# Two sliding-window attention layers, twice: products, sums and places of VectorE and GpSimd assigned anew

## The chip, the cores and the metric

The kernel runs on one core of a Trainium2 chip. The metric is the device time of one execution in microseconds (us). Below, PE is TensorE (matrix products), ACT is ScalarE, DVE is VectorE, POOL is GpSimd, and SP issues the transfers.

## The reference

Four layers act on x of 2048 tokens by 512 features, in the order A, B, A, B, and each adds its result to x. Each starts with a layer norm and ends with a product with its wo. Both layer types have 32 heads of 16 features.

```python
def _A_ref(x, wqkv, wo):                 # W, dil = 8, 2
    idx = pos[:, None] - (jnp.arange(W) * dil)[None, :]
    logits = jnp.einsum("bhsd,bhswd->bhsw", q, kg) * scale
    logits = jnp.where(mask[None, None, :, :], logits, -1e9)
    attn = _softmax(logits, axis=-1)
    o = jnp.einsum("bhsw,bhswd->bhsd", attn, vg)
...
def _B_ref(x, wqkv, wo):                 # W = 256
    scores = jnp.einsum("bhqd,bhkd->bhqk", q, k) * (Dh ** -0.5)
    mask = (idx[:, None] - idx[None, :] >= 0) & (idx[:, None] - idx[None, :] < W)
    p = _softmax(jnp.where(mask[None, None], scores, -1e9), axis=-1)
    o = jnp.einsum("bhqk,bhkd->bhqd", p, v)
...
x = x + _A_ref(_layernorm(x, axis=-1), A_wqkv, A_wo)
x = x + _B_ref(_layernorm(x, axis=-1), B_wqkv, B_wo)
x = x + _A_ref(_layernorm(x, axis=-1), A_wqkv, A_wo)
x = x + _B_ref(_layernorm(x, axis=-1), B_wqkv, B_wo)
```

In a layer A each token attends to 8 tokens, 2 apart. In a layer B it attends to the last 256 tokens.

## The kernel before, in words

The tokens are cut into 8 chunks of 256. A chunk passes through an A layer and then through the next B layer. With two pairs of layers this makes 16 A parts, named A0 to A15, and 16 B parts, B0 to B15. Features lie on the 128 partitions, in four blocks m.

**An A part** (`layer_a`, L836). After the norm and the three projections (L766 to L768), the logits are made in 16 pieces. One `prod` (L893, instruction L895) multiplies q by 8 shifted views of k: 64 tokens by 8 offsets, 512 values on each partition, from SBUF and into SBUF (tile `pr`, four buffers). For each m, four of them feed `reduce_` on PE (L903), which sums over a head's features into the PSUM tile L. `top` (L926, L927) and `bottom` (L930 to L932) on DVE and two steps on ACT make the softmax; `erest` (L940) is the low half of its split into two float16 tiles. Then `spread` (L962) puts the weights on all feature rows in PSUM (tile `pb`), `weigh` (L975, always DVE, 1,024 values) multiplies them by the 8 views of v into tile `pw` (three buffers), and `total` (L977) sums the 8 offsets by three additions in place, L979, L980 and L981, of 512, 256 and 128 values. There are 8 pairs of `weigh` and `total` in an A part. `finish` (L796) splits the sum (L805 on ACT; L807, the low half `ol`), multiplies by wo (L785 to L787) and adds to x (L813).

**A B part** (`layer_b`, L988). Scores go twice through PE. The first time (L1067, L1070) they are there for the row maxima alone, which DVE takes (`top`: L1086 and L1088, or L1081 in a first chunk); `msplit` (L1097, L1098) cuts the maxima in two. The second time (L1140, L1142) they come out transposed, less the maxima, and go to the exponential on ACT (L1146), the mask on POOL (L1155) and the product with v on PE (L1172). Both kinds of scores share two PSUM buffers (`q_sc`). At the end a multiplication of 512 values (L1246) divides by the sums, and `finish` follows.

**The order** is written out in a table. Each step is a task of a `Plan` with an engine and a cost in us. `ORDER` (L40) gives, for each task of each part, its place in its engine's sequence. Four kinds of tasks (`prod`, `total`, `erest`, `ol`) and L1246 have an alternative engine: a negative entry in the table sends the task there. `Plan.order` (L431) runs the sequences against the costs and gives the order in which instructions are emitted, and with it the rotation of the tiles' buffers; each engine keeps the table's order. Tasks of neighbouring parts are mixed: while A4 makes its logits, PE also runs scores of B2 and B3. In the table, DVE has 160 `prod`, POOL 96; POOL has 97 `total`, DVE 31.

In this model of costs a task of mode "S" (a DVE or POOL task between SBUF tiles) is lengthened by 0.7 (DVE) or 0.35 (POOL) of the time that a task of that mode on the other engine lies beside it.

Of the kernel before, what the change touches and what calls it, by code (L numbers as in the profile page):

```python
# [11 lines left out]
F32 = mybir.dt.float32  # L12
# [6 lines left out]
P = 128  # L19
# [21 lines left out]
    "pA": [1, 0, 2, 1, 0, 1, 3, 3, 4, 9, 8, 7, 6, 4, 4, 3, 3, 6, 5, 7, 9, 10, 16, 14, 13, 13, 12, 8, 10, 5, 5, 10, 4,  # L41
        11, 14, 14, 18, 17, 17, 15, 6, 12, 9, 16, 23, 22, 23, 36, 27, 32, 26, 31, 25, 33],
    "pB": [10, 22, 12, 21, 33, 34, 28, 47, 35, 39, 74, 33, 39, 13, 30, 11, 29, 55, 49, 37, 59, 41, 66, 41, 67, 38, 65,
        17, 35, 14, 37, 64, 63, 44, 73, 50, 49, 73, 42, 72, 16, 32, 7, 15, 69, 75, 51, 81, 54, 71, 51, 88, 43, 56, 23,
        24, 44, 15, 20, 21, 19, 18],
    "W": [8, 43, 46, 50, 48, 52, 51, 57, 54, 60, 61, 53, 65, 67, 66, 68, 45, 74, 82, 71, 79, 77, 90, 76, 70, 80, 105,
        88, 96, 91, 83, 102, 104, 99, 97, 106, 101, 108, 84, 113, 98, 109, 112, 111, 100, 103, 166, 169, 181, 190,
        173, 187, 186, 198, 195, 189, 192, 196, 197, 202, 201, 203, 230, 209, 225, 221, 227, 236, 319, 322, 2496,
        2503, 2518, 2522, 2524, 2535, 2531, 2538, 2539, 2546, 2552, 2542, 2554, 2543, 2558, 2563, 2567, 2589, 2596,
        2610, 2609, 2615, 2618, 2632, 2623, 2625, 2622, 2621, 2635, 2628, 2629, 2627, 2624, 2626, 2631, 2634, 2630,  # L50
        2636, 2633, 2645],
    "A0": [0, 1, 0, 1, 2, 2, 2, 6, 5, 8, 7, 11, 9, 2, 0, 11, 12, 13, 19, 20, 21, 25, 27, 20, 23, 15, 16, 17, 18, 24,
        28, 29, 30, 19, 24, 32, 35, 44, 56, 38, 39, 40, 41, 36, 27, 7, 11, 18, -4, -5, 19, 26, 22, 20, -6, 21, 31, -7,
        24, 25, 26, 37, 30, -9, 29, -10, 42, 28, 10, 34, 31, 36, 34, 38, 58, 40, 12, 42, 13, 62, 43, 14, 45, -47, 72,
        48, -50, 47, 16, 78, 52, 18, 53, -56, 40, 17, 85, 86, 87, 89, 58, 44, -58, 92, 93, 94, 95, 61],
    "B0": [59, 62, 21, 64, 46, 110, 48, 69, 45, 107, 47, 68, 115, 117, 120, 122, 114, 116, 118, 119, 54, 77, 52, 75,
        22, 26, 29, 23, 27, 25, 30, 40, 42, 39, 126, 129, 130, 139, 123, 124, 125, 128, 60, 83, 57, 79, 31, 32, 34,
        33, 36, 35, 37, 38, 41, 43, 162, 163, 164, 167, 66, 176, 177, 179, 180, 68, 174, 107, 161, 99, 168, 101, 155,
        96, 153, 92, 170, 103, 159, 97, 175, 105, 108, 184, 114, 45, 212, 73, 204, 70, 35, 220, 206, 71, 217, 74, 36,
        224, 83, 200, 122, 210, 126, 194, 121, 188, 113, 191, 116, 208, 124, 183, 111, 182, 117, 127, 215, 129, 46,  # L60
        235, 80, 231, 78, 40, 252, 258, 88, 266, 91, 42, 289, 101, 234, 141, 241, 147, 216, 131, 228, 138, 226, 137,
        237, 143, 232, 139, 222, 136, 148, 251, 151, 51, 290, 98, 287, 97, 49, 332, 281, 94, 296, 99, 51, 334, 111,
        223, 134, 250, 154, 280, 164, 262, 157, 259, 156, 265, 160, 249, 153, 240, 144, 168, 294, 173, 64, 305, 102,
        302, 100, 52, 310, 311, 109, 318, 108, 54, 329, 110, 67, 66, 72, 73, 204, 74, 75, 212, -66, 122, -216, 363,
        364, 365, 366, 221, 78, 124, 66, 367, 370, 372, 373, 224, 77],
    "A1": [15, 63, 60, 22, 70, 50, 121, 53, 76, 55, 127, 56, 78, 20, 19, 131, 132, 134, 138, 140, 141, 143, 146, 59,
        61, 133, 135, 136, 137, 142, 145, 147, 148, 58, 62, 150, 151, 152, 157, 156, 158, 165, 171, 63, 67, 26, 38,
        82, 81, -25, 80, 144, 86, 87, 84, 85, 149, 90, -26, 89, 91, 154, -28, 93, 94, 95, 160, 98, 64, 100, 65, 102,
        172, 104, 28, 106, 29, 178, 110, 30, 109, -116, 185, 112, 31, 119, 34, 193, 118, 33, 120, -124, 69, 32, 199,
        205, 207, 211, 128, 72, -126, 213, 214, 218, 219, 132],  # L70
    "B1": [130, 133, 39, 135, 75, 229, 77, 140, 76, 233, 79, 142, 239, 243, 246, 247, 238, 242, 244, 245, 84, 152, 81,
        150, 47, 49, 53, 52, 50, 48, 54, 63, 69, 65, 254, 257, 263, 264, 248, 253, 256, 260, 90, 161, 89, 159, 57, 55,
        58, 56, 60, 59, 61, 62, 68, 70, 308, 309, 314, 315, 106, 320, 325, 326, 327, 112, 316, 185, 295, 174, 303,
        179, 291, 171, 286, 169, 306, 181, 312, 183, 321, 188, 189, 331, 193, 71, 347, 118, 337, 114, 61, 351, 340,
        116, 349, 120, 62, 360, 342, 117, 338, 115, 63, 377, 358, 123, 352, 121, 69, 378, 131, 335, 197, 348, 207,
        330, 198, 328, 195, 346, 205, 343, 203, 323, 191, 339, 201, 210, 359, 214, 76, 379, 132, 369, 126, 71, 394,
        374, 130, 385, 133, 72, 396, 416, 146, 392, 135, 74, 431, 393, 136, 406, 142, 75, 438, 153, 362, 218, 388,
        229, 384, 228, 381, 227, 361, 219, 353, 211, 368, 222, 375, 225, 230, 395, 235, 84, 424, 149, 412, 144, 78,
        446, 443, 155, 434, 152, 81, 459, 440, 154, 457, 158, 86, 463, 452, 157, 449, 156, 84, 467, 165, 407, 240,
        397, 237, 417, 245, 433, 254, 425, 248, 430, 249, 398, 238, 411, 243, 255, 445, 258, 99, 461, 161, 464, 162,  # L80
        88, 477, 468, 166, 472, 167, 89, 483, 478, 168, 481, 171, 92, 492, 484, 172, 480, 170, 93, 493, 173, 98, 97,
        106, 105, 288, 107, 108, 295, -104, 184, 105, 524, 525, 526, 527, 305, 110, 186, 107, 528, 532, 533, 534, 307,
        111],
    "A2": [28, 145, 146, 41, 149, 82, 255, 85, 155, 86, 261, 87, 158, 37, 48, 267, 268, 269, 274, 275, 276, 278, 279,
        93, 95, 270, 271, 272, 273, 277, 283, 284, 285, 92, 96, 292, 293, 298, 300, 299, 301, 307, 313, 105, 107, 50,
        64, 163, -45, -44, 162, 282, 166, 167, -46, 165, 288, -48, 172, -47, 170, 297, 178, 175, 177, 176, 304, 180,
        103, 182, 104, 184, 317, 186, 53, 187, 55, 324, 192, 56, 190, -195, 333, 196, 57, 199, 59, 336, 200, 60, 202,
        -207, 113, 58, 341, 344, 345, 350, 209, 119, -209, 354, 355, 356, 357, 216],
    "B2": [213, 217, 68, 220, 125, 371, 127, 223, 128, 376, 129, 226, 382, 386, 390, 391, 380, 383, 387, 389, 137,
        236, 134, 233, 80, 82, 85, 86, 83, 81, 87, 96, 103, 100, 401, 405, 409, 410, 399, 400, 402, 404, 145, 244,  # L90
        141, 242, 90, 88, 91, 89, 93, 92, 94, 95, 101, 102, 462, 470, 474, 475, 169, 482, 486, 489, 494, 175, 473,
        270, 453, 263, 458, 265, 448, 260, 444, 259, 465, 267, 469, 268, 476, 272, 273, 487, 277, 104, 506, 180, 496,
        176, 99, 511, 499, 177, 509, 182, 101, 519, 503, 179, 500, 178, 102, 521, 518, 185, 512, 183, 109, 538, 194,
        495, 282, 508, 291, 491, 281, 488, 279, 505, 289, 501, 287, 485, 276, 497, 284, 293, 520, 299, 109, 539, 193,
        530, 189, 110, 554, 535, 191, 544, 195, 111, 555, 578, 208, 548, 196, 113, 593, 553, 198, 566, 203, 114, 594,
        215, 523, 301, 549, 314, 543, 311, 540, 310, 522, 303, 513, 296, 529, 304, 536, 308, 315, 556, 318, 113, 584,
        211, 572, 206, 118, 606, 603, 217, 596, 212, 122, 618, 595, 216, 616, 221, 124, 626, 612, 219, 609, 218, 123,
        633, 230, 565, 323, 557, 319, 579, 328, 590, 333, 585, 329, 591, 332, 558, 321, 571, 325, 337, 605, 344, 132,
        620, 223, 625, 225, 125, 637, 628, 227, 631, 228, 126, 640, 634, 229, 642, 233, 129, 651, 644, 234, 639, 232,
        130, 654, 235, 131, 130, 137, 138, 371, 139, 141, -141, 378, 246, 143, 684, 685, 686, 687, 388, 143, 248,  # L100
        -385, 689, 692, 693, 694, 391, 144],
    "A3": [79, 232, 231, 73, 234, 138, 403, 139, 239, 140, 408, 143, 241, 67, 70, 413, 414, 419, 423, 422, 427, 428,
        436, 148, 150, 415, 418, 420, 421, 426, 429, 435, 437, 147, 151, 441, 442, 450, 454, 451, 455, 460, 466, 159,
        164, 85, 100, 247, -78, -77, 246, 432, 251, 253, 250, 252, 439, -81, 257, -80, 256, 447, -83, 262, 261, -84,
# [1216 lines left out]
```

## Time and profile before

| | |
|---|---|
| median of 3 runs | 1564.64 us (1563.51 to 1567.54) |
| the profiled execution | 1569.09 us |
| span from its first to its last instruction | 1567.3 us |
| mean granted clock of PE | 0.941 |
| instructions | 35,200 |
| ACT busy | 732.7 us |
| transfers | 96.34 MB, mean 61 GB/s |

The span is what the profile's views cover; the execution's own time is 1.8 us more, and 4.45 us over the median. "Busy" is the time in which an engine runs an instruction. The profile counts a PE instruction as busy over its modelled length, so at a lower granted clock the same work is more busy time.

### The profile page before, as it was taken

What the parts mean: (1) busy time and instruction counts of PE and PEld (TensorE: products, weight loads), DVE (VectorE), ACT (ScalarE), POOL (GpSimd) and SP (SyncE); (2) the same over time, 40 slices, a digit from 0 to 9 for tenths busy, and PEclk for the clock granted to TensorE, in tenths of its full rate; (3) what the DMA queues carried; (4) which work ended last, traced back from release to release, by engine and by line L of the source; (5) the groups of instructions that cost most, each with busy time, mean ns of one, the idle gap of its engine ahead of it and who ended that gap; (6) DMA issues with size and microseconds to landing.
All of it is one profiled execution on the core that took longest, in us unless ns stands there. A gap on an engine that the chain in (4) does not pass through costs nothing.

```text
span 1567.3 us, 35200 instructions
## 1 busy us (share of the span) xinstructions
PE 1419.5 (91%) x14186; PEld 804.5 (51%) x14186; DVE 1295.9 (83%) x2386; ACT 732.7 (47%) x1011; POOL 777.2 (50%) x806
## 2 busy tenths in 40 slices
PE   6899979989899998989899898989989899898988
PEld 4473636446373644636455463735536364463534
DVE  6868797987979798897987979797897979889774
ACT  6432434444445444444455343545444454454554
POOL 3414253654846275573636537363564636547233
PEclk9798999989999999989899898988999899998999
DMA  6130122112130311212122221202212221221211
GB/s 215 28 96 20 62 50 72 48 48 69 50 89 20 96 40 55 79 33 89 29 69 60 60 79 33 88 21 84 54 41 76 50 89 25 64 75 33 82 44 42
DMA packets 73091, 96.34 MB, mean 61 GB/s; under 512 B 17120, under 2 KB 44256, under 8 KB 72928
## 3 DMA queue, kind: packets, MB, share of 16 engines
q1 hardware_dynamic: 72672, 93.83, 21.1%
q8 instruction: 111, 1.82, 0.5%
q14 instruction: 52, 0.43, 0.1%
q10 hardware_dynamic: 256, 0.26, 0.1%
HBM read 49.81 MB, written 34.05 MB: 54 GB/s over the span
## 4 chain that ended last, share of the span: by engine, by line
PE 26%; DVE 16%; issue 3%; POOL 2%; ACT 2%; DMA 2%; SPq 1%; ACTq 0%; DVEq 0%; POOLq 0%
PE av L1172 4%; DVE m L1088 4%; PE pq L766 4%; PE pq L767 3%; PE pq L768 3%; DVE sq L1086 2%; DVE pw L975 2%; PE L L903 2%; PE sk L1140 2%; PE sq L1067 1%; PE po L785 1%; PE po L787 1%; PE po L786 1%; ACT p L1146 1%; PE sq L1070 1%
## 5 line engine op out<-in xcount | busy, mean ns | idle before, releaser
L1146 ACT ACTIVATE p<-sk,sclB 128x768 f32<-128x768 f32 x480 | 428.0, 901 | 358.3 <-PE sk L1142 334.9
L1155 POOL TENSOR_SCALAR_AFFINE_SELECT p<-p 128x1024 f32<-128x1024 f32 x240 | 276.9, 1161 | 420.7 <-ACT p L1146 417.6
L1088 DVE TENSOR_REDUCE m<-sq 128x2 f32<-128x512 f32 x448 | 310.3, 693 | 15.4
L1086 DVE COPY_PREDICATED sq<-maskt,sq 128x256 f32<-128x256 int16 x448 | 188.9, 422 | 99.1 <-PE sq L1070 91.7
L1172 PE MATMUL av<-p,v 128*32 128x256 f32 (+1 forms) x3840 | 211.3, 342 | 4.5 <-POOL p L1155 2.9
L895 POOL TENSOR_TENSOR pr<-kv,q 128x512 f32<-128x512 f32 x96 | 143.9, 1514 | 123.9 <-ACT q L874 69.3
L895 DVE TENSOR_TENSOR pr<-kv,q 128x512 f32<-128x512 f32 x160 | 158.9, 1033 | 34.3 <-ACT q L874 17.4
L1140 PE MATMUL sk<-stk,stk 64*128 64x256 f16 x960 | 138.4, 289 | 40.6 <-DVE m L1088 26.2
L1172 PEld LDWEIGHTS av<-p,v 128*32 128x32 f32 x3840 | 113.9, 112 | 98.5 <-issue 44.5
L975 DVE TENSOR_TENSOR pw<-pb,kv 128x1024 f32<-128x1024 f32 x128 | 152.8, 1212 | 3.0 <-PE pb L962 2.7
L979 POOL TENSOR_TENSOR pw<-pw 128x512 f32<-128x512 f32 x97 | 124.8, 1287 | 54.8 <-DVE pw L975 53.5
L1067 PE MATMUL sq<-stk,stk 48*128 48x128 f16 (+1 forms) x896 | 117.1, 259 | 37.9 <-DVE m L1088 22.9
L1070 PE MATMUL sq<-stk,stk 48*128 48x256 f16 (+1 forms) x1024 | 131.5, 257 | 4.8 <-DVE m L1081 3.3
L1140 PEld LDWEIGHTS <-stk 64*128 64x128 f16 x960 | 53.3, 95 | 152.1 <-issue 93.8
L1067 PEld LDWEIGHTS <-stk 48*128 48x128 f16 x896 | 49.1, 95 | 131.2 <-issue 84.2
L1142 PE MATMUL sk<-stk,stk 64*128 64x128 f16 x960 | 109.8, 225 | 0.0
L737 ACT ACTIVATE xn<-x,rs 128x512 f32<-128x512 f32 x64 | 52.0, 813 | 75.8 <-DVE rs L724 63.9
L903 PE MATMUL L<-pr,sel 128*32 128x512 f32 x512 | 80.5, 603 | 5.3 <-DVE pr L895 4.2
L980 POOL TENSOR_TENSOR pw<-pw 128x256 f32<-128x256 f32 x97 | 74.4, 767 | 7.6
L1207 ACT COPY os<-av 128x512 f32<-128x512 f32 x60 | 35.0, 583 | 85.5 <-PE av L1172 85.3
L766 PE MATMUL pq<-xh,wA1h 128*128 128x256 f16 x256 | 70.1, 274 | 1.8 <-DVE el L1003 1.8
L766 PE MATMUL pq<-xh,wA0h 128*128 128x256 f16 x256 | 70.6, 276 | 0.1
(185 smaller groups left out, 3244.1 us busy)
## 6 DMA issues: line engine op xcount, KB each, us to landing
stk<-re SPq DMA_DIRECT2D x256, 96.0 KB
re<-eh SPq DMA_DIRECT2D x128, 128.0 KB
re<-el SPq DMA_DIRECT2D x64, 128.0 KB
oc<-os SPq DMA_DIRECT2D x120, 64.0 KB
os<-scr SPq DMA_DIRECT2D x15, 512.0 KB
x<-in_A_x_dram SPq DMA_DIRECT2D x8, 512.0 KB
xd<-x SPq DMA_DIRECT2D x16, 256.0 KB
x<-xd SPq DMA_DIRECT2D x8, 512.0 KB
```

The source lines that it names most:

```text
L766: nc.tensor.matmul(ps[mp].t[:, i], wh, xh, start=k == 0, stop=False)
L895: E.tensor_mul(pr.t, window(kv[1].t, m, 64 * tq, 64)[:, 0], qb)
L975: nc.vector.tensor_mul(pw.t, pb.t.unsqueeze(1).broadcast_to([P, 2, W, 64]), v)
L979: E.tensor_add(t[:, :, 0:4], t[:, :, 0:4], t[:, :, 4:8])
L1067: nc.tensor.matmul(ps.t[:, par, 0 : (2 - qb) * P], lhs, stk[hf, bef][r, col, qb * P :], start=True, stop=True)
L1070: nc.tensor.matmul(ps.t[:, par, (2 - qb) * P : 3 * P], lhs, stk[hf, now][r, col, : (1 + qb) * P], start=True, stop=True)
L1086: nc.vector.copy_predicated(t[:, :, 0:P], maskt[:, 0:P].bitcast(I16).unsqueeze(1).broadcast_to([P, 2, P]), t[:, :, 2 * P : 3 * P])
L1088: nc.vector.tensor_reduce(out=m.t[:, qb, :, u], in_=t[:, :, 0 : 2 * P], op=ALU.max, axis=AX.X)
L1140: nc.tensor.matmul(o[:, two], k[:, jf * P : (jf + 1) * P], q, start=True, stop=True)
L1146: nc.scalar.activation(pt.t[:, :, 2 * i : 2 * i + 2].rearrange("p s m q -> p m s q"), ps.t[:, :, : 3 * P].rearrange("p m (s q) -> p m s q" ...
L1155: nc.gpsimd.affine_select(out=v, in_=v, pattern=[[0, 8], [-1 if b == 0 else 1, P]], compare_op=ALU.is_gt if b == 0 else ALU.is_ge, fill=0. ...
L1172: nc.tensor.matmul(o, v[:, jj, 17 * h : 17 * h + 32], rhs, start=z == 0 and (b == 0 or first), stop=z == 1 and b == 1, tile_position=(0, 3 ...
```

## The change

No transfer, no matrix product and no size of a buffer is changed. What is changed:

- **Engines of the tasks with a choice.** The counts over all 16 parts:

| task (line) | DVE before | POOL before | DVE after | POOL after | go POOL to DVE | go DVE to POOL |
|---|---|---|---|---|---|---|
| `prod` (L895) | 160 | 96 | 222 | 34 | 81 | 19 |
| `total` (L979 to L981) | 31 | 97 | 26 | 102 | 1 | 6 |
| `erest` (L940) | 15 | 1 | 7 | 9 | 0 | 8 |
| `ol` (L807) | 21 | 43 | 12 | 52 | 3 | 12 |
| last multiplication (L1246) | 17 | 13 | 24 | 6 | 11 | 4 |

- **The sum on DVE.** Where `total` runs on DVE, it is one reduction of 2 x 64 x 8 values over the offsets and writes the sum at once. On POOL it stays three additions.
- **The table `ORDER`**, with new places for all engines. The parts follow each other as before; of PE's 2,646 tasks 1,787 have another place, by 1.48 places in the mean and 25 at most.
- **The model of costs** that stands behind the table: a DVE task of mode "S" goes on at a rate of 0.33 while any POOL task runs, POOL's is lengthened by 0.25 of the DVE task beside it; some costs are set anew, and `total` and `bottom` no longer have the mode "S". Only the emitted order and the buffers' rotation come from it.
- **Buffers of the products** are handed out by fours: none of the next m before all four of the last.

```diff
 ORDER = {
...
-        1411, 1413, 1423, 1425, 533, 536, 310, 331, -305, 748, -306, 750, 1392, -309, -310, 754, 752, 1401, -312, 757,
...
+        1411, 1420, 1423, 1424, 533, 536, 278, 298, 779, 781, 782, 780, 1391, 785, 786, -276, 787, 1398, 790, 793,
...
-OTHER = {"DVE": "POOL", "POOL": "DVE"}
-SHARE = {"DVE": 0.7, "POOL": 0.35}
+RATE = 0.33
+SLOW = 0.25
...
+                if b.need is None:
+                    taken[b.key] = k = taken.get(b.key, 0) + 1
+                    b.need = (k - 1) // b.group * b.group if b.group else 0
...
+                    if taken[b.key] < b.need:
+                        return math.inf
...
+            if slow is not None:
+                done = RATE * max(0.0, busy - at)
+                end = at + rest / RATE if done >= rest else max(at, busy) + rest - done
...
-            elif e in OTHER and t.mode == "S":
-
-                us += SHARE[e] * max(0.0, min(sbuf[OTHER[e]] - now, us))
-                sbuf[e] = now + us
+            elif e == "POOL":
+                if slow is not None:
+                    k = min(max(busy, at), now)
+                    at, rest = now, max(0.0, rest - RATE * (k - at) - (now - k))
+                    us += SLOW * min(rest, us)
+                busy = now + us
...
-                pr = buf("ppr", [P, W, 64], F32, "pr", f"pr{l}_{c}_{m}_{tq}")
+                pr = buf("ppr", [P, W, 64], F32, "pr", f"pr{l}_{c}_{m}_{tq}", group=4)
...
-                         r=[vq[m // 2], vkv[1][m // 2], vhalo[1]], w=[vpr], mode="S", alt=("POOL", 1.2))
+                         r=[vq[m // 2], vkv[1][m // 2], vhalo[1]], w=[vpr], mode="S", alt=("POOL", 1.3))
...
-        plan.add("DVE", 2.27, bottom, r=[vt1, vmx], w=[ve], mode="S")
+        plan.add("DVE", 2.33, bottom, r=[vt1, vmx], w=[ve])
...
                 def total(E, t0=t0, g=g, pw=pw):
-                    t = pw.t
+                    t, to = pw.t, o.t[:, 2 * g : 2 * g + 2, t0 : t0 + 64]
+                    if E is nc.vector:
+                        E.tensor_reduce(out=to, in_=t.rearrange("p m w t -> p m t w"), op=ALU.add, axis=AX.X)
+                        return
                     E.tensor_add(t[:, :, 0:4], t[:, :, 0:4], t[:, :, 4:8])
                     E.tensor_add(t[:, :, 0:2], t[:, :, 0:2], t[:, :, 2:4])
-                    E.tensor_add(o.t[:, 2 * g : 2 * g + 2, t0 : t0 + 64], t[:, :, 0], t[:, :, 1])
+                    E.tensor_add(to, t[:, :, 0], t[:, :, 1])
...
-                plan.add("POOL", 2.56, total, r=[vpw], w=[vr], mode="S", alt=("DVE", 1.14))
+                plan.add("POOL", 2.5, total, r=[vpw], w=[vr], alt=("DVE", 1.84))
```

The two lines of the table are the same stretch of A9, in which `prod` has 8 negative entries before, five of them in this line, and 1 after.

More of the change, by code (lines that the diff above doesn't have):

```diff
@@ L368, with __init__ @@
 class Buf:
-    def __init__(self, pool, cap, shape, dtype, tag, name):
+    def __init__(self, pool, cap, shape, dtype, tag, name, group=0):
         self.make = lambda: pool.tile(shape, dtype, tag=tag, name=name)
@@ L374, in __init__ @@
         self.left, self.held, self.until = 0, False, 0.0
+        self.group, self.need = group, None
         self.tile = None
@@ L434, in order @@
         slots = {}
+        taken = {}
         for t in self.tasks:
@@ L438, in order @@
                 slots.setdefault(b.key, [0.0] * b.cap)
+                if b.need is None:
+                    taken[b.key] = k = taken.get(b.key, 0) + 1
+                    b.need = (k - 1) // b.group * b.group if b.group else 0
+        taken = dict.fromkeys(taken, 0)
         for q in queue.values():
@@ L441, in order @@
         until = dict.fromkeys(queue, 0.0)
-        sbuf = {"DVE": 0.0, "POOL": 0.0}
+        busy = 0.0
+        slow, at, rest = None, 0.0, 0.0
         dma, mode, tail, use, since = 0.0, "", "", 0.0, 0.0
@@ L447, in begins @@
             t = queue[e][-1]
-            if t.n:
+            if t.n or e == "DVE" and slow is not None:
                 return math.inf
@@ L457, in begins, with leave @@
             return at
+        def leave(t, landed):
+            for x in t.after:
+                x.n -= 1
+                x.ready = max(x.ready, t.end if x.eng == t.eng and not t.size else landed)
+            for b in t.bufs:
+                b.left -= 1
+                b.until = max(b.until, landed)
+                if not b.left:
+                    slots[b.key].append(b.until)
+                    slots[b.key].sort()
         while len(out) < len(self.tasks):
             now, e = min(((begins(e), e) for e in queue if queue[e]), key=lambda x: x[0])
+            if slow is not None:
+                done = RATE * max(0.0, busy - at)
+                end = at + rest / RATE if done >= rest else max(at, busy) + rest - done
+                if end <= now:
+                    slow.end = until["DVE"] = end
+                    leave(slow, end + LAG["DVE"])
+                    slow = None
+                    continue
             if now == math.inf:
@@ L466, in order @@
                     b.held = True
+                    taken[b.key] += 1
                     slots[b.key].pop(0)
@@ L478, in order @@
                 since = now + us
-            elif e in OTHER and t.mode == "S":
-                us += SHARE[e] * max(0.0, min(sbuf[OTHER[e]] - now, us))
-                sbuf[e] = now + us
+            elif e == "POOL":
[4 more added lines that the diff above has]
+                busy = now + us
+            out.append(t)
+            t.start = now
+            if e == "DVE" and t.mode == "S":
+                slow, at, rest = t, now, us
+                continue
             until[e] = t.end = now + us
-            t.start = now
             landed = t.end + LAG[e]
@@ L488, in order @@
                 landed = dma + 0.9
-            for x in t.after:
-                x.n -= 1
-                x.ready = max(x.ready, t.end if x.eng == e and not t.size else landed)
-            for b in t.bufs:
-                b.left -= 1
-                b.until = max(b.until, landed)
-                if not b.left:
-                    slots[b.key].append(b.until)
-                    slots[b.key].sort()
-            out.append(t)
+            leave(t, landed)
         return out
@@ L522, in pool, with buf @@
         pools[name] = ctx.enter_context(tc.tile_pool(name=name, bufs=bufs, **kw)), bufs
-    def buf(name, shape, dtype, tag, label, cap=None):
+    def buf(name, shape, dtype, tag, label, cap=None, group=0):
         p, n = pools[name]
-        return Buf(p, cap or n, shape, dtype, tag, label)
+        return Buf(p, cap or n, shape, dtype, tag, label, group)
     cst = ctx.enter_context(tc.tile_pool(name="cst", bufs=1))
@@ L726, in norm @@
         for t in range(2):
-            plan.add("DVE", 0.91, lambda t=t: stats(t), r=[vx[t]], w=[vmv[t], vr0[t], Val(b6)])
+            plan.add("DVE", 1.0, lambda t=t: stats(t), r=[vx[t]], w=[vmv[t], vr0[t], Val(b6)])
         plan.add("POOL", 0.72, rstd, r=vr0[:2], w=[vr0[2]])
@@ L1197, in leave @@
                         E.dma_start(o_[2 * m + hf :: 8], s_[32 * m : 32 * m + 16])
-                plan.add("DVE", 2.1, divide, r=[vacc], w=[vos[hf][hp], vsh])
+                plan.add("DVE", 2.4, divide, r=[vacc], w=[vos[hf][hp], vsh])
                 for m0, e, E in ((0, "SP", nc.sync), (2, "ACT", nc.scalar)):
@@ L1246, in layer_b @@
             plan.add("DVE", 0.61, lambda E, sl=sl: E.tensor_tensor(out=o.t[:, :, sl], in0=o.t[:, :, sl], in1=os_[1].t[:, :, sl], op=ALU.mult),
-                     r=[vbc, *vog], w=[v], mode="S", alt=("POOL", 1.2))
+                     r=[vbc, *vog], w=[v], mode="S", alt=("POOL", 1.3))
         finish(l, c, o, vo)
```

634 rows, old and new, of the table ORDER are left out of this document.

## The prediction, made before the changed kernel ran

> **What bounds the kernel now.** I read the page's busy times first.
>
> ```profile
> span 1567.3 us, 35200 instructions
> PE 1419.5 (91%) x14186; PEld 804.5 (51%) x14186; DVE 1295.9 (83%) x2386; ACT 732.7 (47%) x1011; POOL 777.2 (50%) x806
> ```
>
> PE looks like the bound, but 91% is a mean over unlike stretches. So I cut each of the 16 A parts at the first and last `prod` and at the last `total`, and asked for busy times by windows. The first stretch I call P (products), the second W (weights and sums), and what is left until the next part's first product R. The columns are the window, its length, then busy time and instructions of PE, PE's weight loads, DVE, ACT and POOL, then PE's granted clock. First P (first window and sum), then W (first and seventh window and sum), then R (sum).
>
> ```profile
> 26.80:41.40 14.60, 14.60 (x105) 8.52 (x103) 13.31 (x25) 5.56 (x8) 9.29 (x7) 1.00 0.26 91
> ...
> sum 274.00, PE 264.15 PEld 163.36 DVE 240.39 ACT 105.82 POOL 192.39; mean PE 16.51 PEld 10.21 DVE 15.02 ACT 6.61 POOL 12.02
> ```
> ```profile
> 41.40:71.30 29.90, 24.39 (x136) 13.58 (x135) 27.69 (x52) 17.07 (x26) 16.65 (x21) 0.74 0.13 36
> ...
> 566.90:602.30 35.40, 29.97 (x322) 12.73 (x324) 33.59 (x52) 17.49 (x23) 25.33 (x28) 0.95 0.16 39
> ...
> sum 549.70, PE 466.39 PEld 196.83 DVE 515.25 ACT 248.24 POOL 372.14; mean PE 29.15 PEld 12.30 DVE 32.20 ACT 15.51 POOL 23.26
> ```
> ```profile
> sum 716.80, PE 675.00 PEld 434.82 DVE 525.12 ACT 357.74 POOL 205.40; mean PE 42.19 PEld 27.18 DVE 32.82 ACT 22.36 POOL 12.84
> ```
>
> In R, PE is busy 675.00 of 716.80 us (94%) and DVE 73%: PE is the bound. In W it is the other way: DVE 515.25 of 549.70 (93.7%), PE 466.39 (85%), and even that at a lowered clock (0.74 in the first window, 0.95 in the one from 566.90, the highest of the 16). A DVE saving in W should therefore become time, and PE has reserves there. P is mixed: PE 264.15 of 274.00 (96%), DVE 88%. What the change is worth lies in P and W.
>
> **The products: 62 more on DVE, 62 fewer on POOL.** The source view of L895 gives ns as min/median/max; then its busy time in P by windows; then the rows by line.
>
> ```profile
> L895 DVE TENSOR_TENSOR pr<-kv,q x160: 660/693/1702, 27.0 to 1399.5; 128x512 f32<-128x512 f32 x160
> L895 POOL TENSOR_TENSOR pr<-kv,q x96: 1166/1628/2903, 26.8 to 1399.0; 128x512 f32<-128x512 f32 x96
> ```
> ```profile
> sum 274.00, DVE 158.47 POOL 143.84; mean DVE 9.90 POOL 8.99
> ```
> ```profile
> L895 POOL TENSOR_TENSOR pr<-kv,q 128x512 f32<-128x512 f32 x96 | 143.9, 1514 | 123.9 <-ACT q L874 69.3
> L895 DVE TENSOR_TENSOR pr<-kv,q 128x512 f32<-128x512 f32 x160 | 158.9, 1033 | 34.3 <-ACT q L874 17.4
> ```
>
> On DVE the same instruction takes 0.66 us at best and 1.70 at worst, with a mean of 1.033 over a median of 0.693: it is held up while POOL works. The excess over the median is 160 x (1.033 - 0.693) = 54.4 us, against 192.4 us of POOL work in P: 0.283 us lost per us of POOL work. Of the 192.4, POOL's products are 143.8. With 34 left at 1.514 each (51.5 us), POOL's work in P is 192.4 - 143.8 + 51.5 = 100.1 us. DVE's products lie beside it more often, by 222/160, so the excess is 100.1 x 0.283 x 222/160 = 39.3 us, and the mean 0.693 + 39.3/222 = 0.870. DVE's product time becomes 222 x 0.870 = 193.1 instead of 160 x 1.033 = 165.3: **+27.8 us on DVE, in P**. The ends: no excess at all (222 x 0.693 = 153.8, or -11.5) and the old mean kept (229.3, or +64.0). I take 0.870, as the overlap with POOL is what the row's spread shows and that is roughly halved.
>
> DVE's work in P is then 240.4 + 27.8 = 268.2. At P's own share (240.4/274) that would take 306 us, at W's share 286. I take W's, since with 14 products to a part instead of 10 there is always one ready: **+12.2 us**.
>
> What waits behind them: in the new table 57 of 66 runs of products on DVE are three or longer, where 23 of 79 were, and a B part's `top` stands behind each run, with PE's two score buffers behind that. PE has projections to run in P (137 half columns of `proj_t`, 138 before), and I let these cover it.
>
> **The sums on DVE: one instruction for three, and five fewer of them.**
>
> ```profile
> L979 DVE TENSOR_TENSOR pw<-pw 128x512 f32<-128x512 f32 x31 | 30.6, 989 | 0.2
> L980 DVE TENSOR_TENSOR pw<-pw 128x256 f32<-128x256 f32 x31 | 29.5, 953 | 1.1
> ...
> L981 DVE TENSOR_TENSOR o<-pw 128x128 f32<-128x128 f32 x31 | 19.0, 614 | 1.1
> ...
> L930 DVE TENSOR_REDUCE mx<-e 128x64 f32<-128x512 f32 x16 | 16.6, 1034 | 1.0 <-ACT e L947 1.0
> ...
> L926 DVE TENSOR_REDUCE mx<-L 128x64 f32<-128x512 f32 x14 | 9.7, 692 | 3.7 <-PE L L903 3.0
> ```
> ```profile
> L1088 DVE TENSOR_REDUCE m<-sq 128x2 f32<-128x512 f32 x448 | 310.3, 693 | 15.4
> ...
> L975 DVE TENSOR_TENSOR pw<-pb,kv 128x1024 f32<-128x1024 f32 x128 | 152.8, 1212 | 3.0 <-PE pb L962 2.7
> ```
>
> A sum costs 0.989 + 0.953 + 0.614 = 2.556 us, 31 of them 79.2. The new instruction's nearest row is L930: it too reduces 8 offsets, 64 values apart, out of SBUF, but 512 values where the sum has 1,024. From L1088 (512 values, 693) to L975 (1,024 values, 1,212) the fixed part of a DVE instruction is about 0.693 - 0.519 = 0.174 us, so I estimate 0.174 + 2 x (1.034 - 0.174) = 1.89 us. The ends are 1.55 (L930's slowness all fixed: 1.034 + 0.519) and 2.07 (twice L930). 26 x 1.89 = 49.2 us: **-29.9 us in W** (-38.9 to -25.4).
>
> The Trainium skill ("VectorE: DVE Perf Modes", on the perf-mode tiers) has `tensor_reduce` at one element per cycle from any memory, and in its rules for kernel authors calls it the slowest DVE operation, to be avoided on a hot path. At L975's rate that would make the sum 1.21 us and DVE's saving some 18 us larger. The trace disagrees for this access from SBUF: L930 takes 1.034 us where L926, of the same shape out of PSUM, takes 0.692.
>
> **The smaller moves.**
>
> ```profile
> L1246 DVE TENSOR_TENSOR oc<-oc,os 128x512 f32<-128x512 f32 x17 | 16.5, 982 | 0.6 <-DMA stk<-re 0.4
> ...
> L940 DVE TENSOR_TENSOR e<-e,eh 128x512 f16<-128x512 f32 x15 | 10.6, 704 | 0.1
> ...
> L807 DVE TENSOR_TENSOR ol<-oc,oh 128x512 f16<-128x512 f32 x11 | 7.9, 717 | 3.8 <-ACT oh L805 3.7
> L807 DVE TENSOR_TENSOR ol<-o,oh 128x512 f16<-128x512 f32 x10 | 6.9, 686 | 0.6 <-ACT oh L805 0.6
> ```
> ```profile
> L807 POOL TENSOR_TENSOR ol<-oc,oh 128x512 f16<-128x512 f32 x21 | 24.8, 1183 | 26.9 <-ACT oh L805 26.6
> ...
> L940 POOL TENSOR_TENSOR e<-e,eh 128x512 f16<-128x512 f32 x1 | 1.2, 1155 | 3.2 <-ACT eh L949 3.2
> ```
> ```profile
> sum 716.80, DVE 16.45 POOL 17.51; mean DVE 1.03 POOL 1.09
> sum 716.80, DVE 14.74 POOL 31.79; mean DVE 0.92 POOL 1.99
> ```
>
> Eight `erest` leave DVE, -8 x 0.704 = **-5.6 us in W**; on POOL each takes 1.155, so the softmax chain is 0.45 longer eight times, 3.6 us if nothing covers it; scores of B do. Nine `ol` fewer (-9 x 0.70 = -6.3) and seven L1246 more (+7 x 0.982 = +6.9) cancel, and lie in R, where DVE has room: the sums over R's windows for L1246 and for L807 are all that DVE does of them. The longer `ol` on POOL (nine times 0.48, 4.3 us) I cost at nothing under PE's work in R. POOL itself loses 62 x 1.514 = 93.9 us and is half idle, so the five more sums there are no term. The model of costs runs before the chip does; the buffers by fours cost nothing, as `reduce_` takes four of one m anyway. The local changes of order, 1.5 places in the mean, I cannot price from rows, on either side; I take zero and let the range hold them.
>
> **The sum.** W: DVE's work is 515.25 - 29.9 - 5.6 = 479.8; at the same 93.7% that takes 511.9 us, -37.8. P: +12.2. R: 0. Together -25.6: the span goes from 1567.3 to 1541.7, and with 1.8 us around it and less the 4.45 by which the profiled execution lies over the median, **1539 us**.
>
> **The rivals.** Shares of time within 0.3% (1560 to 1569) I call no change, about what a measurement here can tell.
>
> *Serial products, slower.* DVE's products keep the old mean of 1.033, since masks and sums now run on POOL beside them, and long runs keep the maxima waiting. P then needs (240.4 + 64.0)/0.937 = 325 us, +51, and with the sum at 2.07 W gives back (515.25 - 25.4 - 5.6)/0.937 = 516.8, -33: +18, or 1583 us. From the break-even on, P is 38 us longer, at 312 us: 292 us of DVE work, a mean product of (292 - 240.4 + 165.3)/222 = 0.98. For it speaks that POOL's masks (L1155) go on in P, against it that they are the smaller part of POOL's work there, 45.40 of 192.39 us:
>
> ```profile
> sum 274.00, POOL 45.40; mean POOL 2.84
> ```
>
>
> *A freed port, faster still.* If a product on either engine shuts out the other's for its whole length, the two engines' products before are 160 x 0.660 + 96 x 1.166 = 217.5 us in a row, and after 222 x 0.660 + 34 x 1.166 = 186.2. Then P falls until PE's 264.15 holds it, -9.9, and with W's -37.8 the time is 1517. The means side by side, 1.033 and 1.514, are both longer than the best cases and both shorter than the two lengths in a row (0.660 + 1.166 = 1.826), which speaks for a partial lock. The Trainium skill ("SBUF — State Buffer", on who interferes with whom) states such a lock, held for the whole instruction by a DVE instruction with two SBUF inputs or by POOL. By that rule this rival is the outcome; the trace bears it out in part, as both operations are lengthened, yet not by each other's full length.
>
> *A reduction as long as the additions.* Beside POOL it costs 2.556 too: 26 x 2.556 = 66.5, so W falls by (12.7 + 5.6)/0.937 = 19.5 only, and the time is 1557.
>
> *No change.* PE holds W after all:
>
> ```profile
> DVE sq L1086 <- PE sq L1070: 91.7, 106, 3.4
> ...
> PE sk L1140 <- DVE m L1088: 26.2, 44, 1.9
> ...
> PE sq L1067 <- DVE m L1088: 22.9, 31, 2.4
> ```
>
> DVE waits 91.7 us in all for scores, so what it saves may become more of such waiting: 1565 us. But PE waits for DVE's maxima too, and the lowered clock in W says that it has nothing to do there.
>
> **How the numbers follow.** Forecast 0.50 (its own range 1524 to 1554), freed port 0.15, long reduction 0.07, no change 0.13, slower 0.15. Faster is 0.50 + 0.15 + 0.07 = 0.72. The range 1512 to 1572 goes below the freed port's 1517 by the shorter reduction's share (26 x (1.89 - 1.55)/0.937 = 9 us at most) and leaves out most of the slower case.
>
> **What would show it.** Right: L895 on DVE x222 with a mean of 0.8 to 0.95; a reduction x26 of 1.6 to 2.0 in place of the three additions; W, cut the same way, near 510 us with a higher clock, and P near 286. Wrong: a product mean near 1.03; W unshortened while L1086 waits longer for PE; or R, on which I count no change, moving by more than 10 us, which would mean that the order rather than the engines made the difference.

## The result and the profile after

The changed kernel takes 1522.28 us, the median of 4 runs (1520.52 to 1524.29), against 1564.43 for the kernel before in the same comparison: a ratio of 0.9728 (95% interval 0.9709 to 0.9746), 42 us less. The profiled execution took 1522.05 us, with a span of 1520.0. The forecast was 1539 us; its rival of the freed port, 1517.

The page's first rows after:

```profile
span 1520.0 us, 35105 instructions
...
PE 1399.7 (92%) x14186; PEld 795.4 (52%) x14186; DVE 1258.1 (83%) x2371; ACT 734.2 (48%) x1011; POOL 682.5 (45%) x769
```

The span is 47.3 us shorter. PE's busy time fell by 19.8 with the same 14,186 matrix products, at a mean granted clock of 0.957 instead of 0.941; the rest, 27.5 us, is idle time of PE that is gone. DVE's work fell by 37.8 us and POOL's by 94.7. The profiled execution of the kernel before lies 4.45 us over its median, so the spans differ by 5 us more than the medians.

The same cut into stretches, from each part's first product to its last product and to the end of its last sum, in sums for P, W and R:

```profile
sum 266.30, PE 262.80 PEld 161.21 DVE 239.51 ACT 105.35 POOL 84.19; mean PE 16.43 PEld 10.08 DVE 14.97 ACT 6.58 POOL 5.26
...
sum 508.30, PE 438.79 PEld 188.23 DVE 480.99 ACT 251.80 POOL 371.47; mean PE 27.42 PEld 11.76 DVE 30.06 ACT 15.74 POOL 23.22
...
sum 718.70, PE 683.84 PEld 436.19 DVE 522.63 ACT 356.30 POOL 219.07; mean PE 42.74 PEld 27.26 DVE 32.66 ACT 22.27 POOL 13.69
```

P went from 274.0 to 266.3 us, W from 549.7 to 508.3, R from 716.8 to 718.7. W lost 41.4 us of length and 34.3 us of DVE's work; R stayed within 2 us. PE's granted clock in the 16 stretches W lies between 0.84 and 0.95, where it lay between 0.74 and 0.95.

The rows of the operations that changed engine, DVE's and then POOL's, and the two rows of `msplit`:

```profile
L921 DVE TENSOR_TENSOR pr<-kv,q 128x512 f32<-128x512 f32 x222 | 164.5, 797 | 30.3 <-ACT q L900 16.0 <-PE L L929 10.1 <-ACT kv L902 3.9
...
L1006 DVE TENSOR_REDUCE o<-pw 128x128 f32<-128x1024 f32 x26 | 50.1, 1926 | 0.2
...
L1126 DVE TENSOR_SCALAR mh<-m 128x16 f16<-128x16 f32 x64 | 22.6, 353 | 1.1
L1127 DVE SCALAR_TENSOR_TENSOR mh<-m,mh 128x16 f16<-128x16 f32 x64 | 20.5, 321 | 2.2
...
L966 DVE TENSOR_TENSOR e<-e,eh 128x512 f16<-128x512 f32 x7 | 4.9, 702 | 0.0
```
```profile
L921 POOL TENSOR_TENSOR pr<-kv,q 128x512 f32<-128x512 f32 x34 | 48.3, 1425 | 42.4 <-PE L L929 25.3 <-PE pm L1131 11.9 <-ACT q L900 5.1
```

62 more products cost DVE only 5.6 us of busy time (158.9 before), since their mean fell from 1.033 to 0.797. Taken one by one in the two traces, the DVE products with no POOL instruction beside them take at most 0.693 us in both kernels; those with one beside them take 1.154 us in the mean before and 1.118 after, but they were 119 of 160 and are 58 of 222. The reduction takes 1.926 us.

The waits that the prediction named, after:

```profile
DVE sq L1115 <- PE sq L1099: 76.6, 94, 3.3
...
PE sq L1096 <- DVE m L1117: 19.0, 34, 2.0
PE sk L1169 <- DVE m L1117: 18.0, 34, 1.9
```

DVE's wait for scores did not grow (91.7 before), and PE waits 12.1 us less for the maxima (49.1 before): the saved DVE time did not turn into waiting.

### The profile page after: what moved, and what is told of

The parts are those of the page before. It is cut to its first block, busy times and chain, and to the rows that moved or that the text cites. A ratio compares the mean times of both kernels' runs of the same rounds, so it can differ in the third digit from the quotient of the medians.

```text
span 1520.0 us, 35105 instructions
## 1 busy us (share of the span) xinstructions
PE 1399.7 (92%) x14186; PEld 795.4 (52%) x14186; DVE 1258.1 (83%) x2371; ACT 734.2 (48%) x1011; POOL 682.5 (45%) x769
## 4 chain that ended last, share of the span: by engine, by line
PE 55%; DVE 19%; issue 4%; ACT 4%; POOL 4%; DMA 3%; SPq 1%; ACTq 0%; POOLq 0%; DVEq 0%
PE pq L792 9%; PE pq L793 7%; PE pq L794 7%; PE av L1201 7%; DVE m L1117 5%; PE sk L1169 4%; PE L L929 4%; DVE sq L1115 3%; PE sq L1096 3%; ACT p L1175 3%; PE po L811 3%; DVE pw L1001 2%; PE po L812 2%; PE po L813 2%; PE sq L1099 2%
## 5 line engine op out<-in xcount | busy, mean ns | idle before, releaser
L1184 POOL TENSOR_SCALAR_AFFINE_SELECT p<-p 128x1024 f32<-128x1024 f32 x240 | 266.4, 1115 | 523.4 <-ACT p L1175 498.8
L1115 DVE COPY_PREDICATED sq<-maskt,sq 128x256 f32<-128x256 int16 x448 | 188.8, 421 | 79.8 <-PE sq L1099 76.6
L1201 PE MATMUL av<-p,v 128*32 128x128 f32 (+1 forms) x3840 | 202.3, 332 | 5.6 <-POOL p L1184 4.9
L921 DVE TENSOR_TENSOR pr<-kv,q 128x512 f32<-128x512 f32 x222 | 164.5, 797 | 30.3 <-ACT q L900 16.0
L1201 PEld LDWEIGHTS av<-p,v 128*32 128x32 f32 x3840 | 108.6, 109 | 89.3 <-issue 33.5
L1008 POOL TENSOR_TENSOR pw<-pw 128x512 f32<-128x512 f32 x102 | 129.7, 1272 | 12.6 <-DVE pw L1001 12.1
L929 PE MATMUL L<-pr,sel 128*32 128x512 f32 x512 | 71.8, 602 | 0.0
L792 PE MATMUL pq<-xh,wA2h 128*128 128x256 f16 x256 | 70.6, 276 | 0.4 <-ACT kv L902 0.2
L792 PE MATMUL pq<-xh,wB1h 128*128 128x256 f16 x256 | 70.8, 277 | 0.0
L793 PE MATMUL pq<-xl,wA0h 128*128 128x256 f16 x256 | 70.5, 275 | 0.4 <-DVE xl L773 0.4
```

Of the source, the lines that this page charges most:

```text
L792: nc.tensor.matmul(ps[mp].t[:, i], wh, xh, start=k == 0, stop=False)
L793: nc.tensor.matmul(ps[mp].t[:, i], wh, xl, start=False, stop=False)
L921: E.tensor_mul(pr.t, window(kv[1].t, m, 64 * tq, 64)[:, 0], qb)
L1115: nc.vector.copy_predicated(t[:, :, 0:P], maskt[:, 0:P].bitcast(I16).unsqueeze(1).broadcast_to([P, 2, P]), t[:, :, 2 * P : 3 * P])
L1184: nc.gpsimd.affine_select(out=v, in_=v, pattern=[[0, 8], [-1 if b == 0 else 1, P]], compare_op=ALU.is_gt if b == 0 else ALU.is_ge, fill=0. ...
L1201: nc.tensor.matmul(o, v[:, jj, 17 * h : 17 * h + 32], rhs, start=z == 0 and (b == 0 or first), stop=z == 1 and b == 1, tile_position=(0, 3 ...
```

## The experiments

Theory E says that each task's price on its engine makes the gain; theory R that the reduction makes most of it; theory O that the new places do. Theory EO, set up after the first four runs, says that engines and places gain only together. In all runs the times of the kernel before come from the same chip, and the ratios are to these.

**The reduction alone.** Two forms. One is the changed program with the old table, and so with the old engines and places:

```diff
 ORDER = {
-    (the table of the changed kernel)
+    (the table of the kernel before)
```

> The changed program with the table ORDER of before, so the engines and sequences of before, with the sum on VectorE in one reduction. Theory E (a task's price on its engine decides: the reduction and the engines carry the gain, the permutations within a part carry under 8 us): the 31 sums on VectorE cost 31 x 1.93 = 59.7 instead of 79.2 us, 19.5 us less work where VectorE is 94% busy, so about 21 us less: 1543 us, ratio 0.987; the products keep their means of 1.03 and 1.5 us. Theory R (the reduction is most of it): 1530 us or less. Theory O (the places found anew are most of it): the shorter sums turn into waits in the old sequence, 1556 us or more.

Measured: 1541.94 us, ratio 0.9839 (0.9823 to 0.9856). As that program also hands out buffers by fours and emits in another order, the other form is the kernel before with nothing but this:

```diff
+                    if E is nc.vector:
+                        E.tensor_reduce(out=to, in_=t.rearrange("p m w t -> p m t w"), op=ALU.add, axis=AX.X)
+                        return
                     E.tensor_add(t[:, :, 0:4], t[:, :, 0:4], t[:, :, 4:8])
```

> The kernel before with the reduction alone; its planner, its costs and its buffers stay. It tells whether the gain of the run with the old table (1542 us, ratio 0.984) was the reduction's or that of the emitted order and the buffers by fours. If the reduction's: within 5 us of 1542. If the buffers': 1555 us or more.

Measured: 1543.36 us, 0.9864 (0.9848 to 0.9881): within 5 us, so the gain is the reduction's; the two intervals overlap, so what the emitted order and the buffers by fours are worth is not settled below some 4 us. Its sums for W and R, by windows, and its row:

```profile
sum 519.80, PE 446.35 PEld 191.16 DVE 493.02 ACT 248.17 POOL 357.68; mean PE 27.90 PEld 11.95 DVE 30.81 ACT 15.51 POOL 22.36
...
sum 719.10, PE 681.49 PEld 437.44 DVE 524.58 ACT 358.23 POOL 205.88; mean PE 42.59 PEld 27.34 DVE 32.79 ACT 22.39 POOL 12.87
```
```profile
L980 DVE TENSOR_REDUCE o<-pw 128x128 f32<-128x1024 f32 x31 | 59.9, 1934 | 0.2
```

31 sums cost 59.9 us for 79.1, 19.2 us less, and W is 29.9 us shorter; P (274.1) and R are not. By the two ratios the reduction alone is worth 25 or 21 us, half of the whole or a little more, so theory R in its strong form (1530 us or less) falls. The reverse, taking it out of the changed kernel:

```diff
-                    if E is nc.vector:
-                        E.tensor_reduce(out=to, in_=t.rearrange("p m w t -> p m t w"), op=ALU.add, axis=AX.X)
-                        return
```

> The changed kernel with the sum on VectorE in three additions again. Theory E: 26 sums at about 2.5 instead of 1.93 us, 15 us more VectorE work in the stretch where VectorE is 95% busy: 1538 us, ratio to the kernel before 0.983. Theory R: 1550 us or more. Theory O: under 8 us more than the changed kernel.

Measured: 1541.12 us, 0.9827 (0.9801 to 0.9854), with four runs from 1534 to 1543 us. By the ratios 26 reductions are worth 15 us there, as theory E expected: the 26 sums in three additions take 27.4 + 21.0 + 17.3 = 65.7 us of DVE's time, for 50.1.

```profile
L1005 DVE TENSOR_TENSOR pw<-pw 128x512 f32<-128x512 f32 x26 | 27.4, 1052 | 0.2
...
L1006 DVE TENSOR_TENSOR pw<-pw 128x256 f32<-128x256 f32 x26 | 21.0, 806 | 0.9
...
L1007 DVE TENSOR_TENSOR o<-pw 128x128 f32<-128x128 f32 x26 | 17.3, 665 | 0.9
```

**Engines and places apart.** Tasks are moved to the other engine at a place in its sequence (the lines shown are those of the old engines in the new sequences):

```diff
+MOVE = {
+    274: ("POOL", 3.76568), 275: ("POOL", 3.65636), 280: ("POOL", 3.875), 283: ("POOL", 3.9375),
...
     both = {"DVE": nc.vector, "POOL": nc.gpsimd}
+    for i, (e, p) in MOVE.items():
+        t = plan.tasks[i]
+        t.eng, t.place = e, p
```

First the new engines in the old sequences ("the one before" in the expectation is the run with the old table):

> As the one before, and each of the 145 tasks with a choice sits on the engine that it has in the changed kernel, put into that engine's old sequence where the planner started it on the other engine; all other places as before. Theory E: within 8 us of the changed kernel, 1514 to 1530 us, with a product on VectorE at a mean near 0.8 us. Theory R: no better than with the reduction alone. Theory O: 1540 us or more, as the moved tasks fall on sequences that are not made for them.

Measured: 1548.17 us, 0.9877 (0.9858 to 0.9896), worse than the reduction without them, as theories R and O have it; theory E excludes it unless the moved tasks stood badly. So the same with searched places:

> The old table with all engines of the changed kernel, as in the run before, but the 145 moved tasks stand at places searched with the kernel's own model of costs; every other task keeps its old place. Theory E (engines): the places of the moved tasks were what was bad, 1530 us or less. Theory EO (engines and places only together): 1535 to 1546 us, as the tasks that were not moved still stand in the old sequence. Theory O: 1546 us or more.

Measured: 1539.71 us, 0.9838 (0.9823 to 0.9853), in theory EO's band and not in theory E's. Then the old engines in the new sequences, the products alone and all 145 tasks:

> The changed kernel with the 100 products that changed engines back on their engines of before (160 on VectorE, 96 on GpSimd), put where the planner started them. Theory E: means near 1.03 and 1.5 us again, the stretch of the products back at 274 us or more, 10 to 20 us more in all: 1532 to 1542 us. Rival (VectorE's work alone counts): its product time falls from 177 to 165 us, so 1522 us or less. Theory O: 1547 us or more.

Measured: 1539.10 us, 0.9822 (0.9808 to 0.9837), in theory E's band; the products' means are 1.052 us on DVE and 1.492 on POOL again, and P takes 282.9 us.

> The changed kernel with all 145 tasks back on their engines of before, at places searched in the same way, everything else in the new sequence, the reduction kept (31 of them). Theory E: 1537 us or more, no better than the old table with the reduction. Theory EO: 1532 to 1542 us, with the stretch of the products at 274 us or more. Theory O: 1527 us or less.

Measured: 1545.82 us, 0.9875 (0.9859 to 0.9891), as theory E has it, and 4 us above the band of theory EO. With the reduction and the planner of the changed kernel in all four, the corners are:

| | old engines | new engines |
|---|---|---|
| old sequences | 0.9839 (0.9823 to 0.9856) | 0.9838 (0.9823 to 0.9853) |
| new sequences | 0.9875 (0.9859 to 0.9891) | 0.9728 (0.9709 to 0.9746) |

The new engines alone bring nothing, the new sequences alone lose 0.4%; both together bring 1.1%, some 17 us. That is theory EO. The lengths of the stretches, in us, cut in the same way:

| | P | W | R |
|---|---|---|---|
| the kernel before | 274.0 | 549.7 | 716.8 |
| old engines, old sequences, with the reduction | 274.2 | 521.2 | 717.9 |
| new engines, old sequences | 270.8 | 521.2 | 718.6 |
| old engines, new sequences | 279.8 | 504.7 | 730.0 |
| the changed kernel | 266.3 | 508.3 | 718.7 |

Of the two mixed corners these are the sums that differ most from the changed kernel: W of the new engines in the old sequences, then P and R of the old engines in the new sequences.

```profile
sum 521.20, PE 447.81 PEld 191.21 DVE 484.14 ACT 247.82 POOL 374.54; mean PE 27.99 PEld 11.95 DVE 30.26 ACT 15.49 POOL 23.41
```
```profile
sum 279.80, PE 275.57 PEld 164.77 DVE 244.16 ACT 109.28 POOL 176.93; mean PE 17.22 PEld 10.30 DVE 15.26 ACT 6.83 POOL 11.06
...
sum 730.00, PE 693.58 PEld 440.71 DVE 527.65 ACT 358.34 POOL 218.26; mean PE 43.35 PEld 27.54 DVE 32.98 ACT 22.40 POOL 13.64
```

The new sequences shorten W by 13 to 16 us and have fewer matrix products begin there: 4,235 with the old table, 4,103 with the old engines in the new sequences, 4,148 in the changed kernel. With the old engines, P and R grow by as much as W loses; with the new ones they do not. One limit stays: the moved tasks' places were searched with the kernel's model of costs, not on the chip, so a better old sequence for the new engines may exist. Which of the changed places carry the 17 us stays open.

**What the products cost each other.** The kernel before, with POOL's products made cheap:

```diff
+                    if E is nc.gpsimd:
+                        E.memset(pr.t, 0.0)
+                        return
                     E.tensor_mul(pr.t, window(kv[1].t, m, 64 * tq, 64)[:, 0], qb)
```

> The kernel before, with GpSimd's 96 products replaced by filling the tile with zeros: left out is that part of the logits. It takes GpSimd's reads and half of its time out of the stretch of the products, and touches nothing else. Lock theory (the two engines' products shut each other out and so set that stretch): the mean of VectorE's product falls from 1.03 to 0.8 us or less, the stretch from 274 to 262 us or less, the time to 1545 to 1556 us. Rival (TensorE holds that stretch): the mean falls, the stretch and the time stay, 1560 us or more.

Measured: 1544.70 us, 0.9858 (0.9844 to 0.9873), just under the band of the lock theory. DVE's row, and the sums of P cut at DVE's first and last product, of the kernel before and then of this run:

```profile
L898 DVE TENSOR_TENSOR pr<-kv,q 128x512 f32<-128x512 f32 x160 | 114.4, 756 | 44.6 <-PE L L906 21.2 <-ACT q L874 19.2 <-ACT kv L876 2.8
```
```profile
sum 265.30, PE 255.67 PEld 157.24 DVE 236.49 ACT 102.41 POOL 184.35; mean PE 15.98 PEld 9.83 DVE 14.78 ACT 6.40 POOL 11.52
```
```profile
sum 238.90, PE 235.86 PEld 148.96 DVE 188.85 ACT 96.21 POOL 81.25; mean PE 14.74 PEld 9.31 DVE 11.80 ACT 6.01 POOL 5.08
```

The same 160 DVE products take 114.4 instead of 158.9 us, and P, cut alike, shrinks from 265.3 to 238.9, though PE was 96% busy there: the products held P. PE's own busy time fell with it by 19.8 us, while of its 2,794 matrix products 2,697 still begin there, so a busy PE was no floor. The run takes away POOL's own product time along with the contention, so it does not split the two. The same edit in the changed kernel asks what is left:

> The changed kernel with its 34 products on GpSimd replaced by filling with zeros, that part of the logits left out. It bounds what these products still cost. Lock theory: 34 of them lie mostly beside VectorE's; the mean falls from 0.80 to 0.74 us, 13 us of VectorE's work, but TensorE is 99% busy in that stretch, so 0 to 6 us less than 1522. If more than 8 us less, the contention is still a bound.

Measured: 1521.69 us, 0.9719 (0.9693 to 0.9746), no different from the changed kernel. And the last 34 products on DVE:

> The changed kernel with the last 34 products on VectorE too, at places searched with the kernel's own model of costs, everything else in place. 34 more products at 0.69 add 23 us of work to VectorE and take about 13 us of contention from it; TensorE is 99% busy in that stretch and VectorE 90%: within 5 us of 1522 either way. Faster than 1517 would say that the lock still costs more than the work; slower than 1530 that VectorE has become the bound there.

Measured: 1525.06 us, 0.9733 (0.9718 to 0.9747): no change either. Their DVE rows:

```profile
L924 DVE TENSOR_TENSOR pr<-kv,q 128x512 f32<-128x512 f32 x222 | 147.9, 722 | 35.9 <-ACT q L900 16.3 <-PE L L932 15.4 <-ACT kv L902 3.9
```
```profile
L931 DVE TENSOR_TENSOR pr<-kv,q 128x512 f32<-128x512 f32 x256 | 168.8, 716 | 35.6 <-ACT q L910 18.8 <-PE L L939 12.8 <-ACT kv L912 3.5
```

Even with 16.6 us less product work on DVE the time does not move now: the contention in P is no bound of the changed kernel.

**The contention by itself.** Two kernels without any attention; in each stretch DVE repeats one operation on its own tiles while POOL repeats another.

```python
for mine in (prod, reduce_, adds):
    for other in (None, mask, prod, adds):
        meet()
        if other is not None:
            for i in range(pool_reps[other]):
                other(nc.gpsimd, "p", i)
        for i in range(REPS if mine is not adds else 6):
            mine(nc.vector, "d", i)
```

> No attention: VectorE repeats the product, the reduction and the three additions on tiles of its own, each beside nothing, beside GpSimd's mask, product and three additions on other tiles, then GpSimd alone; the output is a copy of x. Lock for the whole instruction: beside GpSimd's product VectorE's product takes about 0.69 + 1.17 = 1.86 us, and GpSimd's as long. Partial lock: 1.2 to 1.6 us and 1.5 to 1.7. The reduction: 1.93 us beside each of them if it never contends, over 2.2 if it does. The three additions: 1.40 us alone and 2.4 to 3 beside GpSimd.

In this first one the framework mixed the stretches, so it gives no means, but its timeline has the single cases (start, duration, both in us):

```profile
45.34 1.09 POOL L66 TENSOR_SCALAR_AFFINE_SELECT pt<-pt 128x1024 f32<-128x1024 f32 x1
45.39 1.58 DVE L53 TENSOR_TENSOR prd<-kvd,qd 128x512 f32<-128x512 f32 x1
46.40 1.61 POOL L53 TENSOR_TENSOR prp<-kvp,qp 128x512 f32<-128x512 f32 x1
46.90 1.90 DVE L56 TENSOR_REDUCE od<-pwd 128x128 f32<-128x1024 f32 x1
47.97 1.08 POOL L66 TENSOR_SCALAR_AFFINE_SELECT pt<-pt 128x1024 f32<-128x1024 f32 x1
```

DVE's product begins 0.05 us after the mask and ends 0.54 after the mask's end at 46.43. POOL's product begins at 46.40 and ends 1.04 after DVE's end at 46.97. Alone they take 0.69 and 1.18, so each does nearly all its work after the other has finished, and 0.15 us of it before. The reduction runs through with 1.90 us, and the mask beside it with 1.08. The second kernel has the order written out:

```diff
     cst = ctx.enter_context(tc.tile_pool(name="cst", bufs=1))
+    ctx.enter_context(tc.manual_schedule())
```

> As the first side run, in the order written, so that each operation of VectorE runs in a stretch of its own beside one of GpSimd's; no attention, the output is a copy of x. The first run showed a product of 0.68 us alone, 1.58 to 1.67 where GpSimd's instruction had begun just before, and the reduction at 1.86 to 1.91 whatever ran beside it. Whole-instruction lock: products in a row on both engines take turns, so each engine gets one done in 1.7 to 1.9 us, and beside masks one in 1.6 to 1.8. Partial sharing: under 1.5. The reduction 1.85 to 1.95 beside everything, and GpSimd's operations beside it as long as alone.

Its rows by window: DVE's product alone; DVE's product beside masks; both engines' products; the reduction alone; the reduction beside POOL's products.

```profile
L54 DVE TENSOR_TENSOR prd<-kvd,qd 128x512 f32<-128x512 f32 x12 | 8.3, 691 | 0.4
```
```profile
L67 POOL TENSOR_SCALAR_AFFINE_SELECT pt<-pt 128x1024 f32<-128x1024 f32 x14 | 19.1, 1364 | 0.9
L54 DVE TENSOR_TENSOR prd<-kvd,qd 128x512 f32<-128x512 f32 x11 | 15.3, 1389 | 0.4
```
```profile
L54 POOL TENSOR_TENSOR prp<-kvp,qp 128x512 f32<-128x512 f32 x9 | 13.6, 1508 | 0.7
L54 DVE TENSOR_TENSOR prd<-kvd,qd 128x512 f32<-128x512 f32 x8 | 12.4, 1552 | 0.3
```
```profile
L57 DVE TENSOR_REDUCE od<-pwd 128x128 f32<-128x1024 f32 x13 | 24.4, 1874 | 0.4
```
```profile
L57 DVE TENSOR_REDUCE od<-pwd 128x128 f32<-128x1024 f32 x12 | 22.7, 1893 | 0.4
L54 POOL TENSOR_TENSOR prp<-kvp,qp 128x512 f32<-128x512 f32 x14 | 16.5, 1181 | 1.0
```

In a row the two engines' products take turns: one of each in about 1.55 us, where alone they take 0.69 and 1.18. That lies between the two bands: less than 0.69 + 1.18 = 1.87 by 0.3, which is what the two overlaps of 0.15 in the first side run give, and far more than the longer of them. Beside masks a product takes 1.39 us, under the expected 1.6 to 1.8, and the mask is lengthened too, from 1.09 to 1.36. DVE alone makes 12 products in 8.3 us, 1.4 per us; both engines together make two in 1.55 us, 1.3 per us. For products in a row the help of the second engine is worth less than nothing. The reduction is not touched, and does not touch POOL (its product alone: 1.175 us). The three additions take 1.41 us alone, 2.9 beside POOL's additions and 3.6 beside its products, the latter over the expected 2.4 to 3.

## Why the prediction was right in direction and too small

The time fell by 42 us, by 25.6 in the forecast, and 1522 lies in the range though outside the likeliest case's own 1524 to 1554. On the span, P missed by -20 us, W by -4 and R by +2.

- **W is bound by DVE: right.** The sums fell from 79.1 to 50.1 us, -29.0 against -29.9 forecast, at 1.926 us each against the estimate of 1.89; `erest` -5.7 against -5.6. DVE's work in W is 481.0 us, 479.8 forecast, and W 508.3, 511.9 forecast. DVE is busy 95% of W (94% before). The size is partly luck: with the same engines and the reduction in the old sequences W took 521.2 us, so 13 us of W's saving need the new sequences, which the forecast had at zero.
- **The Trainium skill's rate for the reduction ("VectorE: DVE Perf Modes", on the perf-mode tiers): the measurement stands.** 1.874 us alone and undisturbed, not the 1.21 of one element per cycle at `weigh`'s rate.
- **P gets longer by 12.2 us: wrong**; it got 7.7 shorter, and this is nearly the whole miss. The step that failed is the product's mean of 0.870 and, from it, 27.8 us more DVE work. The mean was 0.797; the excess over 0.693 came to 222 x 0.104 = 23 us, not 39. I had let it grow with the number of DVE's products and shrink with POOL's work, as if both were strewn at random. In fact the products that meet a POOL instruction fell from 119 of 160 to 58 of 222; the new engines in the old sequences already bring them to 76. I also compared counts times means (165.3, and 176.9 after) with stretches of busy time, in which instructions overlap at their ends (158.9, and 164.5 after). DVE's work in P stayed at 239.5 us, as `msplit`, which I had left out, fell there from 9.5 to 5.7. W's share of 93.7% for P was too high too: P kept 90%.
- **R unchanged: right.** It moved by 1.9 us, so this sign of the order does not show; yet the order does matter, as the next point says.
- **The changed places at zero: wrong.** With the engines and the reduction in place, the new sequences are the difference between 0.9838 and 0.9728, 17 us. Of the 42 us about 25 are the reduction's, and the other 17 need engines and sequences together.
- **The rivals.** The freed port came nearest, with -47.7 on the span against -47.3 measured: P -9.9 against -7.7, W -37.8 against -41.4. Its mechanism is what the side kernels show, and so the Trainium skill's rule ("SBUF — State Buffer", on who interferes with whom), that the port is held for a whole instruction, agrees with this trace up to the 0.3 us that a pair saves; the same section's statement that a reduction never contends agrees too (1.893 us beside POOL's products, 1.874 alone). Its floor for P, PE's 264 us, was no floor: with POOL's products made cheap PE's busy time in P shrank along with P, from 255.7 to 235.9. The agreement is thus partly luck. The long reduction, the return of the saving as waits and the serial products are refuted by the 1.926 us, by the 76.6 us of DVE's wait and by the mean of 0.797.

## What to carry to other kernels

Before work is shared between VectorE and GpSimd, measure a pair side by side: for operations with two SBUF inputs the second engine can take more than it gives. The better neighbours on VectorE are those that are not held up: the reduction, and `weigh` with one operand from PSUM (1.159 to 1.226 us in the kernel before, with or without GpSimd at work). Engines and sequences have to be found together: here neither alone gained anything, and both together 17 us. A stretch in which TensorE is 96% busy need not be bound by it; take away the other engine's work once and see whether the stretch shrinks.

## What the runs showed of the hardware

- A reduction over 8 values 256 bytes apart takes 1.87 us for 1,024 values from SBUF; three additions of 512, 256 and 128 values do the same in 1.41 us undisturbed (0.691 + 0.426 + 0.292 in the side kernel). It wins only where GpSimd is at work beside it: there the additions took 2.56 us in the kernel before.
- A small instruction can be held up for many times its own length: of the 64 of `msplit`'s first, 16 values each, the 30 with no GpSimd instruction beside them take at most 0.176 us in the kernel before, the 34 others 0.659 in the mean and 1.157 at worst. The source view of all 64, in ns as min/median/max:

```profile
L1097 DVE TENSOR_SCALAR mh<-m x64: 160/175/1157, 130.4 to 1537.9; 128x16 f16<-128x16 f32 x64
```
